# A Fourier layer and eight experts on one core: another order of the experts' model and inner dimensions

## The chip, the cores and the metric

The kernel runs on one core of one Trainium2 chip. The core has a matrix engine (TensorE, PE in the profile, with PEld for its weight loads), a vector engine (VectorE, DVE), a scalar engine (ScalarE, ACT), a general engine (GpSimd, POOL) and a queue that only issues DMAs (SyncE, SP). Matrix products land in PSUM; everything else lies in SBUF, which has 128 partitions. Each engine works through its own list of instructions in a fixed order, and waits for the others by semaphores. The metric is the device time of one execution in microseconds; the time before is the median of three runs.

## What is computed

The reference has two halves. The first mixes a batch of 8 sequences (2496 positions, 256 features) in the frequency domain; the second routes all 19968 tokens to 8 experts of equal capacity and applies each expert's two-layer network.

```python
X = np.fft.rfft(x, axis=1); Xr, Xi = X.real, X.imag
Yr = Xr @ w_r - Xi @ w_i + b_r
Yi = Xr @ w_i + Xi @ w_r + b_i
Yr = sign(Yr) * max(|Yr| - 0.01, 0); Yi = sign(Yi) * max(|Yi| - 0.01, 0)
x = np.fft.irfft(Yr + 1j * Yi, n=2496, axis=1).reshape(19968, 256)

logits = x @ w_gate                          # [19968, 8]
# all (token, expert) pairs in order of falling logit: a token goes to the first
# expert that still has room; each expert takes cap = 19968 / 8 = 2496 tokens
for e in range(8):
    h = np.maximum(x[assigned == e] @ w1[e], 0.0)    # w1[e]: 256 x 1024
    out[assigned == e] = h @ w2[e]                   # w2[e]: 1024 x 256
```

The product of an expert doesn't depend on the order in which the 256 features of x and w1's rows are summed, nor on the order in which the 1024 inner columns are numbered, as long as w1's columns and w2's rows are numbered alike.

## The kernel before

**Stages.** The transform runs batch by batch (`phase_a`), as matrix products with fixed matrices, with transposing steps through DRAM (T1, T2); its result goes to the DRAM tensor YD and its logits to LG. When four batches are done, a router (`Router.early`) finds for each expert up to 512 tokens that will surely be its own: the eight *early lists*. Their experts' products run at the end of the transform and behind it. When all logits are there, `Router.closing` finds, one expert after the other, the expert whose capacity closes next, and the rest of its tokens (1984): the eight *late lists*. Each closing is a search for a threshold: DVE counts (L402 to L407), PE sums the counts over partitions (L412, L413), DVE decides (L430 to L434, L451, L452). There is a slow way, `general`, for inputs on which the certificates of the fast way fail; it isn't run with these inputs.

**A list's work** (`Experts.run`). Tokens are gathered from YD by an indirect DMA (L581), 128 at a time, a token to a partition. `xpose` turns them by PE (L596), so that features lie on partitions: the 256 features are two groups of 128, and the transposing matmul's weight load reads one group of columns. ACT and DVE split the result into a high and a low part (L599, L600). `ffn1` makes the hidden layer, 128 inner columns (ft) and up to 512 tokens at a time, from three products: high times high, high times low, low times high (L611), summed over the two groups of features. ACT and DVE apply the maximum and split again (L614, L615). `ffn2` sums over the eight ft (L627), ACT copies (L630), and an indirect DMA scatters the rows to the output (L634).

**A list's weights** (`Experts.load`). Each of w1 and w2 of an expert comes in two halves of 512 KB into a raw tile of 128 partitions x 1024 words. There are two raw tiles; they lie where the transform had its tile xt, so the profile names them xt. For each half, ACT copies the raw words into the high part (L567) and DVE subtracts the copy from the raw words into the low part (L568), which also frees the raw tile for the next half. w1's parts lie in tiles that the profile names sh, w2's in FG; each has two places, so that one list's weights can be made while another's are in use. Early lists know their expert, and SP loads the halves by plain DMAs (L557). Late lists' experts are known only from the search, so POOL gathers 128 rows of 4 KB by row numbers that DVE makes (wi, L809 to L811), with an indirect DMA (L559); the same two columns of row numbers serve w1 and w2.

**The numbering before.** Half m of w1 has the rows d = 2 p + m on partition p, each 1024 columns long, 4 KB. Inner column f = 8 k + t becomes place k of ft = t, so the two split instructions read the raw row with a step of eight words and write in order. w2's rows f = 8 p + t belong to that: half g has rows 8 p + 4 g to 8 p + 4 g + 3, 4 KB in one piece, in order. The transposes read every second column of the gathered tokens.

**What sets the order.** A planner (`Plan.run`) simulates the whole program with given costs and positions and writes out each engine's order once, at build time. Its costs are numbers in the calls: 0.95 us for the ACT copy (L567) and 0.068 + 1024/960 us for the DVE subtraction (L568), 0.118 us for a transpose, 0.65 us and a tail for a DMA from SP. PE's order thus has the search's little matmuls at fixed places between the experts' matmuls, and DVE's order has the search's counts at fixed places between the experts' splits.

Of the kernel before, what the change touches and what calls it, by code (L numbers as in the profile page):

```python
# [15 lines left out]
OP = mybir.AluOpType  # L16
# [250 lines left out]
class Kit:  # L267
# [17 lines left out]
    def v(self, n, pos, emit, reads, writes): return self.plan.add('V', 0.068 + n / 960, pos, emit, reads, writes)  # L285
# [252 lines left out]
class Experts:  # L538

    def __init__(self, K, H, YD, YDb, w1, w2, out):  # L540
        self.K, self.H, self.YD, self.YDb, self.out = K, H, YD, YDb, out
        self.w = (w1, w2)
        self.rows = (w1.rearrange("e (p m) f -> (e p m) f", m=2), w2.rearrange("e (p g m) d -> (e p g) (m d)", g=2, m=4))
        self.spacer = K.one("spacer_b", [1, 1])
        self.scat = []

    def load(self, pos, e=None, wi=None):

        K, plan, v = self.K, self.K.plan, self.K.v
        W1, W2 = K.sb("W1", [128, 2, 2, 1024], F32R), K.sb("W2", [128, 2, 8, 256], F32R)  # L550
        for k in range(2):
            for m in range(2):
                r = K.sb("raw", [128, 1024])
                p = pos + (2 * k + m)
                if e is not None:
                    src = self.w[k][e].rearrange("(p m) f -> p m f", m=2)[:, m] if not k else self.w[k][e].rearrange("(p g m) d -> p g (m d)", g=2, m=4)[:, m]
                    K.dma(p, lambda r=r, src=src: K.nc.sync.dma_start(r.t, src), 524e3, [], [r])  # L557
                else:
                    K.ind(p, lambda r=r, k=k, m=m: K.P.indirect_dma_start(out=r.t, out_offset=None, in_=self.rows[k],  # L559
                                                                          in_offset=bass.IndirectOffsetOnAxis(ap=wi.t[:, m:m + 1], axis=0)), 524e3, [wi], [r])  # L560

                def part(i, k=k, m=m, r=r):
                    if k: return W2.t[:, i - 1, 4 * m:4 * m + 4] if i else r.t.rearrange("p (m d) -> p m d", m=4)
                    return W1.t[:, i - 1, m].rearrange("p (t k) -> p t k", t=8) if i else r.t.rearrange("p (k t) -> p t k", t=8)
                W = (W1, W2)[k]
                h = plan.buf(None, None)
                plan.add('A', .95, p + 1, lambda part=part: K.A.copy(part(1), part(0)), [r], [W, h])  # L567
                v(1024, p + 1, lambda part=part: K.V.tensor_tensor(part(2), part(0), part(1), op=OP.subtract), [r, h], [W])  # L568
        return W1, W2

    def run(self, n, base, W, gi, go, gs, oi, oo, pos_g, early=False):

        K, H, plan, v = self.K, self.H, self.K.plan, self.K.v
        V, A, P, T = K.V, K.A, K.P, K.T
        W1, W2 = W
        NT, NC = (n + 127) // 128, (n + 511) // 512
        xg, xT, hT = {}, {}, {}
        for t in range(NT):
            if not t % 2: xg[t // 2] = K.sb("xg", [128, 2, 256])
            g = xg[t // 2]  # L580
            q = K.ind(pos_g(t), lambda t=t, g=g: P.indirect_dma_start(  # L581
                out=g.t[:, t % 2], out_offset=None, in_=self.YD[0:EB * S] if early else self.YD, in_offset=bass.IndirectOffsetOnAxis(ap=gi.t[:, go + t:go + t + 1], axis=0)),
                131e3, [gs[t]] + (self.YDb[0:EB] if early else self.YDb), [g])
            gi.users.append(q)

        def xpose(c, pos):
            nt = min(4, NT - 4 * c)
            xT[c] = [[K.sb("xT", [128, 512], F32R) for _ in range(2)] for _ in range(2)]
            for m in range(2):
                h, l = xT[c][m]  # L590
                ps = K.psum("psx", [128, 512])

                def tr(ps=ps, m=m):
                    for q in range(nt):
                        t = 4 * c + q
                        T.transpose(ps.t[:, 128 * q:128 * q + 128], xg[t // 2].t[:, t % 2].rearrange("p (k m) -> p m k", m=2)[:, m], H.idn)  # L596
                K.t(.118 * nt, pos + .5 * m, tr, [H.b_idn] + [xg[t] for t in range(2 * c, 2 * c + (nt + 1) // 2)], [ps])
                w = 128 * nt
                plan.add('A', .052 + w / 1200, pos + .5 * m, lambda ps=ps, h=h: A.copy(h.t[:, 0:w], ps.t[:, 0:w]), [ps], [h])  # L599
                v(w, pos + .5 * m, lambda ps=ps, h=h, l=l: V.tensor_tensor(l.t[:, 0:w], ps.t[:, 0:w], h.t[:, 0:w], op=OP.subtract), [ps, h], [l])  # L600
# [39 lines left out]
        HD, k = 2, base  # L640
# [32 lines left out]
class Router:  # L673
# [56 lines left out]
    def closing(self, i, pos, lo3):  # L730

        K, H, X = self.K, self.H, self.X
        V, T, v = K.V, K.T, K.v
# [4 lines left out]
        ML, m, am, AG, eid, certs, lohi = H.b_ML, H.b_m, H.b_am, H.b_AG, H.b_eid, H.b_certs, H.b_lohi  # L738
# [3 lines left out]
        if i < 7:  # L742
# [14 lines left out]
            rng, r = self.rng, RR[i]  # L757
# [3 lines left out]
            else:  # L761
# [4 lines left out]
                ps = count(K, H, pos, c, no, ag, NJ, "pq", self.junk, self.acc, eqs)  # L766
# [8 lines left out]
            ps = count(K, H, pos, c, no, ag, NJ, "pq", self.junk, self.acc, eqs)  # L775
            f = self.fl[i] = K.sb("fl", [128, 8])
# [6 lines left out]
            wf, g8 = K.sb("wi", [128, 1]), K.sb("g8", [128, 8])  # L783
            v(8, pos(), lambda: V.scalar_tensor_tensor(g8.t[:, 0:no], f.t[:, 0:no], 1.0, eid.t[:, 0:no], op0=OP.mult, op1=OP.mult, accum_out=wf.t), [f, eid], [g8, wf])
            pw = pos()
# [16 lines left out]
        else:  # L802
            wf, pw = K.sb("wi", [128, 1]), pos()
# [2 lines left out]

        v(215, pos(), lambda: V.scalar_tensor_tensor(gl.t, gm.t, 1.0, H.ne, op0=OP.mult, op1=OP.mult, accum_out=cnt.t[:, 0:1]), [gm, H.b_ne], [gl, cnt])
        wa, wi = K.sb("wi", [128, 1]), K.sb("wi", [128, 2], I32)
        v(1, pw, lambda: V.tensor_scalar(wa.t, wf.t, 7.0, 128.0, op0=OP.min, op1=OP.mult), [wf], [wa])  # L809
        v(1, pw, lambda: V.tensor_tensor(wa.t, wa.t, H.pc[:, 0:1], op=OP.add), [wa, H.b_pc], [wa])  # L810
        v(2, pw, lambda: V.scalar_tensor_tensor(wi.t, wa.t.to_broadcast([128, 2]), 2.0, H.iE[:, 0:2], op0=OP.mult, op1=OP.add), [wa, H.b_iE], [wi])  # L811
        ps2 = K.psum("pq", [128, 8])
        K.t(.05, pos(), lambda: (T.matmul(ps2.t[:, 0:1], lhsT=H.tri, rhs=cnt.t[:, 0:1], start=True, stop=True), T.matmul(ps2.t[:, 1:2], lhsT=H.ones, rhs=cnt.t[:, 0:1], start=True, stop=True)), [cnt, H.b_tri, H.b_ones], [ps2])
        v(1, pos() + 5, lambda: V.tensor_scalar(certs.t[:, 8 + i:9 + i], ps2.t[:, 1:2], 1.0 - CAP + EN, None, op0=OP.add), [ps2], [certs])
# [7 lines left out]
        p = pos() + 5  # L822
# [337 lines left out]
def general(tc, nc, H, LG, YD, w1, w2, cR, out):  # L1160
# [4 lines left out]
    with ExitStack() as ctx:  # L1165
        K = Kit(tc, nc, ctx, RINGS)
        plan, V, A, P, T, v, sb, psum = K.plan, K.V, K.A, K.P, K.T, K.v, K.sb, K.psum
# [3 lines left out]
        pc, iE, ones, tri, sml, ML, m, am, AG = H.b_pc, H.b_iE, H.b_ones, H.b_tri, H.b_sml, H.b_ML, H.b_m, H.b_am, H.b_AG  # L1171
# [25 lines left out]
        def closing(i, pos):  # L1197
# [7 lines left out]
            if i < 7:  # L1205
# [31 lines left out]
                for k in range(31, -1, -1):  # L1237
# [10 lines left out]
                    ps = total(cnt)  # L1248
# [5 lines left out]
                ps = total(cnt)  # L1254
# [8 lines left out]

            g8, wf, wi = sb("g8", [128, 8]), sb("wi", [128, 1]), sb("wi", [128, 2], I32)
            v(8, pos(), lambda g8=g8, wf=wf: V.scalar_tensor_tensor(g8.t, wE.t, ec.t[:, 0:1], iE.t, op0=OP.is_equal, op1=OP.mult, accum_out=wf.t), [wE, ec, iE], [g8, wf])
            v(1, pos(), lambda wf=wf: V.scalar_tensor_tensor(wf.t, wf.t, 128.0, pc.t[:, 0:1], op0=OP.mult, op1=OP.add), [wf, pc], [wf])
            v(2, pos(), lambda wf=wf, wi=wi: V.scalar_tensor_tensor(wi.t, wf.t.to_broadcast([128, 2]), 2.0, iE.t[:, 0:2], op0=OP.mult, op1=OP.add), [wf, iE], [wi])
            if i < 7:

                g8a, g8b, g8c = [sb("gw", [128, 8]) for _ in range(3)]  # L1270
# [95 lines left out]
```

## Time and profile before

| | |
|---|---|
| median of three runs | 1635.14 us (1633.94 to 1639.24) |
| the profiled execution | 1637.3 us, span 1635.5 us, mean granted clock 0.984 |
| PE busy | 1543.4 us, 94% of the span |
| DVE busy | 1181.4 us, 72% |
| ACT busy | 882.4 us, 54% |
| POOL busy | 607.8 us, 37% |
| DMA | 210.64 MB, mean 129 GB/s |

One execution was profiled, and its lines are quoted by engine (PE, PEld, DVE, ACT, POOL, SP), source line and the names of the tiles written and read ("sh<-xt" is w1's split). Buffer numbers are left out of the names. "PE a L1 <- DVE b L2: 8.4, 6, 2.3" says that PE stood idle in front of its instructions on tile a at line 1 for 8.4 us in all, six times, at most 2.3 us, until DVE's instruction on b at line 2 ended. A q behind an engine's name means its instruction queue. Matmuls overlap one another, so PE's busy time is a union of overlapping spans.

### The profile page before, as it was taken

How to read it: one execution, taken by the hardware profiler on the slowest of the kernel's cores; microseconds unless marked ns; L12 is line 12 of the kernel's file. 1: busy time of each engine (PE TensorE's matmuls, PEld its weight loads, DVE VectorE, ACT ScalarE, POOL GpSimd, SP SyncE). 2: the span in 40 equal slices, each digit the busy share in tenths (PEclk: the TensorE clock that was granted, in tenths of full speed). 3: DMA queues.
4: the chain of work that ended last, by engine and by line, in shares of the span. 5: the costliest groups of instructions: out<-in, count | busy, mean ns of one | idle time of the engine just before them, and what ended most of it. 6: DMA issues, size and time to landing. Idle time of an engine off the chain costs nothing.

```text
span 1635.5 us, 31215 instructions
## 1 busy us (share of the span) xinstructions
PE 1543.4 (94%) x10980; PEld 1381.9 (84%) x10980; DVE 1181.4 (72%) x3652; ACT 882.4 (54%) x1875; POOL 607.8 (37%) x726
## 2 busy tenths in 40 slices
PE   6999999999999967989899999999999999999997
PEld 3899999998798845878788888888889899889997
DVE  2777777778988885688988989988777766552331
ACT  1568788787688764454634434444344443563331
POOL 1114343343344556212342623534325253473112
PEclk8999999999999988999999999999999999999999
DMA  8877787887686564323221302211122211231000
GB/s 239 237 248 249 224 248 221 251 248 204 216 235 223 165 186 139 113 90 105 90 79 44 101 25 72 71 67 61 44 75 70 72 61 62 84 115 46 20 25 27
DMA packets 134489, 210.64 MB, mean 129 GB/s; under 512 B 31183, under 2 KB 94367, under 8 KB 134129
## 3 DMA queue, kind: packets, MB, share of 16 engines
q1 hardware_dynamic: 112468, 145.53, 29.7%
q0 software_dynamic: 21856, 63.04, 12.3%
q8 instruction: 88, 1.44, 0.4%
q14 instruction: 77, 0.63, 0.1%
HBM read 123.75 MB, written 84.75 MB: 127 GB/s over the span
## 4 chain that ended last, share of the span: by engine, by line
PE 31%; issue 12%; DVE 6%; POOL 4%; ACT 2%; DMA 2%; POOLq 0%; ACTq 0%
PE ps L627 14%; PE ps L611 10%; PE p L611 5%; POOL out_dram L634 3%; DMA xt<-in_moe_w_dram,wi 2%; DVE sh L568 2%; ACT sh L567 1%; PE ps L596 1%; DVE junk L402 1%; DVE FG L568 1%; ACT FG L567 0%; PE p L499 0%; POOL xt L559 0%; DVE yTl L615 0%; ACT ajunk L504 0%
## 5 line engine op out<-in xcount | busy, mean ns | idle before, releaser
L1010 PE MATMUL ps<-wt,xTh 128*128 128x256 f32 x1280 | 242.9, 289 | 0.0
L1010 PEld LDWEIGHTS ps<-wt,xTh 128*128 128x128 f32 x1280 | 200.8, 192 | 2.9 <-issue 0.2
L1010 PE MATMUL ps<-wt,xTl 128*128 128x256 f32 x640 | 181.3, 283 | 0.0
L868 POOL TENSOR_TENSOR s2l<-s2c,s2h 120x512 fp32r<-120x512 f32 (+1 forms) x96 | 118.0, 1233 | 142.7 <-ACT s2h L865 136.5
L634 POOL DMA_INDIRECT out_dram<-xTh,li x64 | 71.2, 1113 | 263.1 <-ACT xTh L630 235.5
L1087 POOL TENSOR_TENSOR yTl<-yr,yTh 128x468 bf16<-128x468 f32 (+1 forms) x88 | 98.8, 1122 | 165.8 <-ACT yTh L1084 114.9
L402 DVE SCALAR_TENSOR_TENSOR junk<-h_m,st,h_AG 128x156 bf16<-128x156 f32 (+1 forms) x472 | 157.9, 380 | 2.5
L1010 PEld LDWEIGHTS ps<-wt,xTl 128*128 128x128 f32 x640 | 122.2, 191 | 0.0
L630 ACT COPY xTh<-ps 128x256 f32<-128x256 f32 x80 | 29.9, 373 | 149.1 <-PE ps L627 127.3
L627 PE MATMUL ps<-FG,yTh 128*128 128x256 f32 (+1 forms) x504 | 108.8, 283 | 0.0
L991 PE MATMUL ps<-FG,sh 128*128 128x128 f32 x640 | 97.0, 282 | 8.4 <-DMA sh<-T 8.0
L991 PEld LDWEIGHTS ps<-FG,sh 128*128 128x128 f32 x640 | 88.4, 195 | 16.5 <-issue 9.5
L630 ACT COPY xTl<-ps 128x256 f32<-128x256 f32 x80 | 29.8, 372 | 126.7 <-PE ps L627 120.6
L634 POOL DMA_INDIRECT out_dram<-xTl,li x64 | 64.9, 1014 | 86.8 <-ACT xTl L630 77.8
L627 PE MATMUL ps<-FG,yTl 128*128 128x256 f32 (+1 forms) x368 | 88.3, 283 | 0.0
L568 DVE TENSOR_TENSOR sh<-xt,sh 128x1024 fp32r<-128x1024 f32 x32 | 69.4, 2182 | 17.9 <-ACT sh L567 17.8
L627 PEld LDWEIGHTS ps<-FG,yTh 128*128 128x128 f32 (+1 forms) x504 | 80.7, 187 | 0.7
L627 PE MATMUL ps<-FG,s2c 128*128 128x256 f32 (+1 forms) x356 | 80.4, 284 | 0.0
L1016 DVE TENSOR_TENSOR ps<-ps,bt 128x512 f32<-128x512 f32 x80 | 55.5, 694 | 30.7 <-PE ps L1010 25.6
L868 DVE TENSOR_TENSOR xl<-xt,xh 117x512 fp32r<-117x512 f32 (+1 forms) x77 | 61.0, 794 | 22.3 <-ACT xh L865 20.2
L1057 PE MATMUL p<-s2h,d 120*117 120x512 f32 (+1 forms) x192 | 76.7, 408 | 0.3 <-DVE s2h L865 0.3
L611 PE MATMUL ps<-y,sh 128*128 128x512 f32 (+1 forms) x187 | 71.5, 400 | 3.6 <-DVE yTl L615 1.6
(648 smaller groups left out, 5162.8 us busy)
## 6 DMA issues: line engine op xcount, KB each, us to landing
sh<-T SPq DMA_DIRECT2D x40, 512.0 KB
T<-s4st SPq DMA_DIRECT2D x80, 256.0 KB
s2c<-T SPq DMA_DIRECT2D x80, 240.0 KB
YD<-yst SPq DMA_DIRECT2D x80, 234.0 KB
T<-s1st SPq DMA_DIRECT2D x73, 240.0 KB
xt<-in_moe_w_dram SPq DMA_DIRECT2D x32, 512.0 KB
xt<-in_x_dram SPq DMA_DIRECT2D x105, 156.0 KB
LG<-lgst SPq DMA_DIRECT2D x80, 21.9 KB
```

What stands on the lines that cost most here:

```text
L402: v(cols + 59, p, lambda k=k: V.scalar_tensor_tensor(junk[k % 2].t[:, 0:cols], H.m[:, 0:cols], c.t[:, k // ng:k // ng + 1], ag(k % ng)[:, ...
L568: v(1024, p + 1, lambda part=part: K.V.tensor_tensor(part(2), part(0), part(1), op=OP.subtract), [r, h], [W])
L611: T.matmul(ps.t[:, 0:w], lhsT=W1.t[:, a, m, 128 * ft:128 * ft + 128], rhs=x_.t[:, 0:w], start=q + m == 0, stop=q + m == 3)
L627: T.matmul(ps.t[0:M], lhsT=a.t[:, 128 * q:128 * q + M], rhs=W2.t[:, w_, ft], start=k == 0, stop=k == 23)
L630: plan.add('A', .27, pos + 1, lambda: A.copy(o.t[0:M], ps.t[0:M]), [ps], [o])
L634: ins = P.indirect_dma_start(out=self.out, out_offset=bass.IndirectOffsetOnAxis(ap=oi.t[0:M, oo + t:oo + t + 1], axis=0), in_=o.t[0:M], in ...
L868: lambda: eng.tensor_tensor(lb[1](), src(), hb[1](), op=OP.subtract), [srcb, hb[0]], [lb[0]])
L991: T.matmul(ps.t[:, i, 128 * dt:128 * dt + 128], lhsT=sh.t[:, k, 128 * dt:128 * dt + 128], rhs=Ft.t[:, k], start=True, stop=True)
L1010: T.matmul(ps3.t[:, i], lhsT=a.t[:, i, dt, o:o + 128], rhs=wt[c].t[:, w, dt], start=n == 0, stop=n == 11)
L1016: plan.add('V', dve(512), pos + 1.282, lambda ps3=ps3: V.tensor_tensor(ps3.t, ps3.t, bt[:, None, :].to_broadcast([128, 2, 256]), op=OP.add ...
L1057: T.matmul(ps.t[0:M, gs_], lhsT=d5[0:k_, a, 0:M], rhs=v.t[0:k_, gs_], start=i == 0, stop=i == 2)
L1087: yq.append(plan.add('P', pool(2 * W), pos + 0.376, lambda yh=yh, yl=yl, yr=yr, W=W: P.tensor_tensor(yl.t[:, :, 0:W], yr.t[:, :, 0:W], yh. ...
```

## The change

Model dimension: half m has the features d = 128 m + p, in place of 2 p + m. Transposes read 128 neighbouring columns; w1's halves are blocks of 128 neighbouring rows.

Inner dimension, late lists: f = 512 g + 4 k + t is place k of ft = 4 g + t. The gathered row of w2, four rows of 1 KB in one piece of 4 KB, is row number 128 g + p of an expert's 256; the split of w1 reads its raw row with a step of four words. So the row number is 256 e + 128 m + p for both weights, made by three instructions as before.

Inner dimension, early lists: in memory order, f = 512 g + 128 t + k. The split of w1 reads its raw row in order; a half of w2 is loaded as four pieces of 1 KB for each partition, rows 512 g + 128 t + p, by the same DMA from SP.

The planner's costs and positions stay. The same edit of the row numbers is made in `general`.

```diff
-        self.rows = (w1.rearrange("e (p m) f -> (e p m) f", m=2), w2.rearrange("e (p g m) d -> (e p g) (m d)", g=2, m=4))
+        self.rows = (w1.rearrange("e d f -> (e d) f"), w2.rearrange("e (r m) d -> (e r) (m d)", m=4))
...
-                    src = self.w[k][e].rearrange("(p m) f -> p m f", m=2)[:, m] if not k else self.w[k][e].rearrange("(p g m) d -> p g (m d)", g=2, m=4)[:, m]
-                    K.dma(p, lambda r=r, src=src: K.nc.sync.dma_start(r.t, src), 524e3, [], [r])
+                    src = self.w[k][e].rearrange("(m p) f -> p m f", m=2)[:, m] if not k else self.w[k][e].rearrange("(g m p) d -> p g m d", g=2, m=4)[:, m]
+                    K.dma(p, lambda r=r, src=src, k=k: K.nc.sync.dma_start(r.t.rearrange("p (m d) -> p m d", m=4) if k else r.t, src), 524e3, [], [r])
...
-                    return W1.t[:, i - 1, m].rearrange("p (t k) -> p t k", t=8) if i else r.t.rearrange("p (k t) -> p t k", t=8)
+
+                    return W1.t[:, i - 1, m].rearrange("p (g t k) -> p g t k", g=2, t=4) if i else r.t.rearrange("p (g k t) -> p g t k" if e is None else "p (g t k) -> p g t k", g=2, t=4)
...
-                        T.transpose(ps.t[:, 128 * q:128 * q + 128], xg[t // 2].t[:, t % 2].rearrange("p (k m) -> p m k", m=2)[:, m], H.idn)
+                        T.transpose(ps.t[:, 128 * q:128 * q + 128], xg[t // 2].t[:, t % 2, 128 * m:128 * m + 128], H.idn)
...
-        v(1, pw, lambda: V.tensor_scalar(wa.t, wf.t, 7.0, 128.0, op0=OP.min, op1=OP.mult), [wf], [wa])
+        v(1, pw, lambda: V.tensor_scalar(wa.t, wf.t, 7.0, 256.0, op0=OP.min, op1=OP.mult), [wf], [wa])
         v(1, pw, lambda: V.tensor_tensor(wa.t, wa.t, H.pc[:, 0:1], op=OP.add), [wa, H.b_pc], [wa])
-        v(2, pw, lambda: V.scalar_tensor_tensor(wi.t, wa.t.to_broadcast([128, 2]), 2.0, H.iE[:, 0:2], op0=OP.mult, op1=OP.add), [wa, H.b_iE], [wi])
+        v(2, pw, lambda: V.scalar_tensor_tensor(wi.t, H.iE[:, 0:2], 128.0, wa.t.to_broadcast([128, 2]), op0=OP.mult, op1=OP.add), [wa, H.b_iE], [wi])
```

More of the change, by code (lines that the diff above doesn't have):

```diff
@@ L1265, in closing @@
             v(8, pos(), lambda g8=g8, wf=wf: V.scalar_tensor_tensor(g8.t, wE.t, ec.t[:, 0:1], iE.t, op0=OP.is_equal, op1=OP.mult, accum_out=wf.t), [wE, ec, iE], [g8, wf])
-            v(1, pos(), lambda wf=wf: V.scalar_tensor_tensor(wf.t, wf.t, 128.0, pc.t[:, 0:1], op0=OP.mult, op1=OP.add), [wf, pc], [wf])
-            v(2, pos(), lambda wf=wf, wi=wi: V.scalar_tensor_tensor(wi.t, wf.t.to_broadcast([128, 2]), 2.0, iE.t[:, 0:2], op0=OP.mult, op1=OP.add), [wf, iE], [wi])
+            v(1, pos(), lambda wf=wf: V.scalar_tensor_tensor(wf.t, wf.t, 256.0, pc.t[:, 0:1], op0=OP.mult, op1=OP.add), [wf, pc], [wf])
+            v(2, pos(), lambda wf=wf, wi=wi: V.scalar_tensor_tensor(wi.t, iE.t[:, 0:2], 128.0, wf.t.to_broadcast([128, 2]), op0=OP.mult, op1=OP.add), [wf, iE], [wi])
             if i < 7:
```

## The prediction

> **What bounds the kernel now.** The page first: its span and the chain that ended last.
>
> ```profile
> span 1635.5 us, 31215 instructions
> PE ps L627 14%; PE ps L611 10%; PE p L611 5%; POOL out_dram L634 3%; DMA xt<-in_moe_w_dram,wi 2%; DVE sh L568 2%; ACT sh L567 1%; PE ps L596 1%; DVE junk L402 1%; DVE FG L568 1%; ACT FG L567 0%; PE p L499 0%; POOL xt L559 0%; DVE yTl L615 0%; ACT ajunk L504 0%
> ```
>
> The chain ends in the experts' matmuls (L611, L627), but "DVE sh L568" and "ACT sh L567" stand in it: the two instructions that split w1 (tile sh) into a high and a low part. The split of w2 (tile FG), of the same size, is at 1% and 0%. So I asked for both lines by form.
>
> ```profile
> L567 ACT CAST sh<-xt x32: 2075/2246/2431, 505.1 to 1426.7; 128x1024 fp32r<-128x1024 f32 x32
> L567 ACT CAST FG<-xt x32: 1037/1048/1112, 570.1 to 1447.1; 128x1024 fp32r<-128x1024 f32 x32
> L568 DVE TENSOR_TENSOR sh<-xt,sh x32: 2003/2186/2354, 507.3 to 1429.0; 128x1024 fp32r<-128x1024 f32 x32
> L568 DVE TENSOR_TENSOR FG<-xt,FG x32: 1205/1225/1950, 574.6 to 1448.2; 128x1024 fp32r<-128x1024 f32 x32
> ```
>
> The same 128x1024 takes 2.25 us on ACT for w1 and 1.05 for w2, on DVE 2.19 and 1.23 (medians). The only difference is the pattern read: w2 in memory order, w1 every eighth word (f = 8 k + t), 32 bytes apart. Each of the 16 lists splits w1 in two halves: 16 halves belong to early lists, 16 to late ones.
>
> Then the stages, by stretches of the span (columns: length, then busy time of PE, weight loads, DVE, ACT, POOL, granted clock, DMA share, GB/s).
>
> ```profile
> 470.00:560.00 90.00, 85.46 (x718) 78.84 (x717) 74.55 (x156) 70.25 (x166) 49.82 (x46) 1.00 0.73 223
> 560.00:640.00 80.00, 58.99 (x409) 44.62 (x409) 62.49 (x112) 47.78 (x104) 48.19 (x42) 0.87 0.53 157
> 640.00:830.00 190.00, 172.75 (x1133) 151.78 (x1132) 153.99 (x537) 98.24 (x162) 58.83 (x79) 0.98 0.33 106
> 830.00:886.00 56.00, 54.97 (x369) 48.61 (x368) 46.67 (x247) 18.86 (x35) 13.90 (x23) 1.00 0.11 35
> 886.00:1480.00 594.00, 581.62 (x3916) 522.23 (x3915) 450.43 (x1804) 270.53 (x640) 253.23 (x332) 1.00 0.22 71
> ```
>
> From 640 to 830, where early lists 3 to 8 run and the first late list gets its weights, PE is idle 190 - 172.75 = 17.25 us. From 830 on it has next to no gap: 1.0 us to 886, and 12.4 in 594 us of late lists. What PE waits for from 640 to 830 (total us, times, longest):
>
> ```profile
> PE pt L412 <- DVE cnt L407: 8.4, 6, 2.3
> PE ps L627 <- DVE zh L615: 3.2, 2, 1.6
> PE ps L627 <- DVE yst L615: 2.8, 2, 1.6
> ```
>
> That is 14.4 of the 17.25 us in ten waits, all for small DVE work that is queued on DVE. What it is queued behind, at one of them (timeline of ACT, DVE, PE):
>
> ```profile
> 696.68 4.58 ACT L567 CAST sh<-xt 128x1024 fp32r<-128x1024 f32 x2 [0.93 <-PE p L611]
> 699.07 4.34 DVE L568 TENSOR_TENSOR sh<-xt,sh 128x1024 fp32r<-128x1024 f32 x2 [1.25 <-ACT sh L567]
> 704.42 0.16 DVE L407 TENSOR_TENSOR cnt<-acc,cnt 128x4 bf16<-128x4 f32 x1
> 704.64 0.18 PE L412 MATMUL pt<-cnt,h_ones 128*128 128x4 bf16 x1 [2.34 <-DVE cnt L407]
> ```
>
> DVE waits 1.25 us for the first ACT copy, then splits two halves for 4.34 us; the router's count comes out at 704.58, and PE, which has the count's matmul next in its order, stands 2.34 us. So in this stage the split of w1 is what ends last, at seven pairs: early lists 3 to 8, and late list 1 near 815. (Early list 1 splits at 505 to 516, list 2 at 588 to 596, late list 2 near 891 and so on.)
>
> **The change, part by part.** No duration given to the planner changes, so every engine keeps its order and no instruction or DMA is added, dropped or moved past a queue. Only durations change.
>
> *w1, early lists: read in memory order.* By the rows of FG, the first ACT copy falls by 2.25 - 1.05 = 1.20 us and the two DVE subtractions by 0.96 each: a pair ends 1.20 + 1.92 = 3.1 us sooner. The longest PE wait is 2.3 us, so each that stands behind an early pair should close. Six of the seven pairs are early; the late one keeps its wait of up to 2.3 us, and I leave 1 us to waits that only happen to end on L407: 11 of the 14.4 us, about the DVE work that goes, 6 x 1.92 = 11.5. Bounds: 6 us (every second copy decides, 6 x 0.96) and 15 (all of PE's idle time but the late wait). What is late next is PE itself, at its matmul rate. Of early list 1 I count nothing, since 470 to 560 has 4.5 us of PE gaps in all. List 2's is on the way to the last logits (timeline of DVE, then PE's waits):
>
> ```profile
> 591.48 4.12 DVE L568 TENSOR_TENSOR sh<-xt,sh 128x1024 fp32r<-128x1024 f32 x2
> 595.52 0.63 DVE L1082 TENSOR_TENSOR yr<-pt,yTh 128x468 f32<-128x468 f32 x1
> PE ps L1098 <- POOL yTl L1087: 1.9, 1, 1.9
> PE ps L1098 <- ACT yTh L1084: 1.4, 1, 1.4
> ```
>
> PE's gate matmuls wait 3.3 us there for work queued behind these copies; DVE gives back 1.9 us. I take 2 (bounds 0 and 3.3).
>
> The gain must pass the stretch 830 to 886. Its last event is the number of the second late list's expert, from a search in which DVE and PE answer each other (DVE's waits from 830 to 890, and POOL's timeline):
>
> ```profile
> DVE g L451 <- PE pt L413: 8.2, 11, 1.2
> 886.50 0.98 POOL L559 DMA_INDIRECT xt<-in_moe_w_dram,wi  x1 [7.99 <-DVE wi L811]
> ```
>
> DVE is busy 46.67 of 56 us there and waits 8.2 for PE, while PE waits for almost nothing: PE sets the pace, and if both come to 830 earlier, all of it is earlier.
>
> *w1, late lists: f = 512 g + 4 k + t, words 16 bytes apart.* No row has this pattern. Its bounds are the two forms above: 2.25 and 2.19 us, or 1.05 and 1.23. A wider stride stands in the maximum over lists, 624 bytes:
>
> ```profile
> L747 DVE TENSOR_REDUCE h_m<-h_ML 128x156 f32<-128x1092 f32 x1 | 2.3, 2314 | 0.0
> L747 DVE TENSOR_REDUCE h_m<-h_ML 128x156 f32<-128x936 f32 x1 | 2.0, 2005 | 0.0
> ```
>
> (2314 - 2005)/156 = 1.98 ns a word, against 2186/1024 = 2.13 at 32 bytes: from 32 to 624 bytes the price stands still, like a fixed price for leaving the neighbourhood of the last word. The nearest row is the 32-byte one, so I take no gain; the other bound is a rival. [...] No run here shows 16 bytes.
>
> *Transposes (L596), 320: columns 128 m on, no longer every second.* The weight load reads them:
>
> ```profile
> L596 PEld LDWEIGHTS ps<-h_idn,y 128*128 128x128 f32 x56 | 9.4, 209 | 0.6 <-issue 0.2
> L991 PEld LDWEIGHTS ps<-FG,sh 128*128 128x128 f32 x640 | 88.4, 195 | 16.5 <-issue 9.5 <-DMA sh<-T 0.8 <-PE p L960 0.8
> ```
>
> 14 ns dearer than L991, which reads neighbours. 320 x 14 ns = 4.5 us at most; loads overlap matmuls, so nothing at least. I take 2, nearly all in the PE-bound stage.
>
> *w2, early lists: four pieces of 1 KB for each of 128 partitions, no longer 4 KB.* 16 DMAs go from 128 pieces to 512. SP's issue price for 512 pieces stands at L351, beside L557's own; then a pair's issue and its use, and the DMA rate where such 4 KB loads run and where the transform's 1 KB rows (T, s2c, YD) do.
>
> ```profile
> L351 SPq DMA_DIRECT2D h_ML<-LG x8: 585/589/687, 180.1 to 650.3; - x8
> L557 SPq DMA_DIRECT2D xt<-in_moe_w_dram x32: 327/328/367, 479.9 to 786.3; - x32
> 675.28 2.36 SPq L557 DMA_DIRECT2D xt<-in_moe_w_dram  x2
> 686.18 2.00 ACT L567 CAST FG<-xt 128x1024 fp32r<-128x1024 f32 x2 [3.14 <-PE ps L627]
> DMA to landing us min/median/max: 3.9/4.8/5.8
> 663.00:668.00 5.00, 4.85 (x25) 3.97 (x24) 4.83 (x12) 2.76 (x7) 3.75 (x4) 1.00 0.65 210
> 240.00:260.00 20.00, 20.00 (x166) 18.78 (x165) 16.93 (x30) 15.52 (x34) 6.57 (x5) 1.00 0.83 229
> ```
>
> SP pays 0.26 us more for each; behind the pair of list 3 (647 us) stand the last batch's logits (L351), 0.5 us later by that and 3.1 sooner because the raw tiles come free sooner. At 210/0.65 = 323 GB/s of full share against 229/0.83 = 276, a pair of 1.05 MB takes 0.5 us longer. It is issued by 677.64 and used at 686.18, released by PE: 8.5 us, where the late lists' loads of the same 512 KB land in 5.8 at most. Covered; cost 0. Without the cover it would be 0.5 to 1 us a list.
>
> *The row numbers (L809 to L811)* are the same three small DVE instructions, with other factors: 0. The late w1 gather fetches 128 neighbouring rows of 4 KB, no longer every second: 0, within the 3.9 to 5.8 us above.
>
> **Sum:** 11 + 2 + 2 = 15 us; by the bounds 6 to 23. The profiled execution took 1637.3 us around its span of 1635.5; 1637.3 - 15 = 1622.3. The median shown, 1635.14, is 2.2 below that execution, so 1620.
>
> **The rivals.** *(a) 16 bytes are as cheap as neighbours.* Then the late lists' pairs also end 3.1 us sooner: 2.3 us at late list 1, and of the 12.4 us of PE gaps among the others, some of which are for transfers and for ACT, 8 us: 1610. For it: nothing here has a stride between 8 and 32 bytes. Against: the flat price from 32 to 624. [...]
>
> *(b) The gain is swallowed at 886.* If the search's DVE work, and not PE, sets the second late list's number, PE arrives 13 us early and stands until the gather at 886. Left are the transposes and little else, 3 us: 1632. For it: DVE is 81% busy from 640 to 830, and busy or waiting all the time from 830. Against: what DVE waits for there is PE, and DVE itself loses 11.5 us of work before 830.
>
> *(c) Slower: the early w2 loads become the bound.* If a piece costs the same whatever its size, a pair takes four times as long on the DMA engines: 1.05 MB at 323 GB/s is 3.3 us, so 13, landing near 690 where ACT wants it at 686 or, sooner now, 683; 4 to 7 us late for six lists is 24 to 42, less 15: about 1653. It decides from 8.5 us between issue and landing on. Against: the row at 240 us, where 1 KB rows move at 276 GB/s of full share.
>
> That memory order doesn't speed the split is hardly a case: FG is the same copy.
>
> **How the numbers follow.** Forecast 57% (own range 1612 to 1629, the bounds), (a) 25%, (b) 13%, (c) 5%. The range runs from 1606 ((a) with all its 14.7 us) to 1631, leaving out (c) and most of (b). About 0.3% (4.9 us) is what can be told from no change here. Faster: 57 + 25 and 3 of (b), 85%; same 10%; slower 5%.
>
> **What would show it.** L567 and L568 on sh should fall apart into 16 at 1.05 and 1.23 us and 16 at about 2.2. PE's idle time in the early stage should fall from 17 to about 6 us, its waits for cnt L407 almost vanish, and the second late list's first gather be issued near 873, not 886.5; the late lists from there should keep their length to 2 or 3 us. Wrong would be: the gather still at 886; sh at 16 bytes below 1.5 us; ACT FG released by a DMA in the early stage; L596 loads still at 209 ns.

## The result and the profile after

The changed kernel takes 1616.59 us (median of four runs, 1611.52 to 1618.58), where the kernel before takes 1635.14. The ratio is 0.9875, with a 95% interval from 0.9855 to 0.9895: faster, by 18.5 us or 1.2% between the medians. The profiled execution took 1618.58 us, 18.7 less than that of before (1637.3).

The page of the changed kernel (its lines are numbered one higher from L567 on: L568 is ACT's copy, L569 DVE's subtraction, L597 the transposes, L612 and L628 the experts' matmuls):

```profile
span 1616.8 us, 31215 instructions
DMA packets 140633, 210.64 MB, mean 130 GB/s; under 512 B 31183, under 2 KB 102559, under 8 KB 140273
PE ps L628 20%; PE ps L612 13%; PE ps L1011 11%; PE p L612 6%; PE ps L992 3%; PE ps L1028 3%; PE p L961 3%; PE p L1058 2%; POOL out_dram L635 2%; DMA xt<-in_moe_w_dram,wi 2%; PE ps L597 1%; PE pt L1078 1%; DVE junk L402 1%; DMA sh<-in_x_dram 1%; DVE sh L569 1%
```

The chain still ends in the experts' matmuls, now with more of them in it; "ACT sh" has left the list and "DVE sh" is down from 2% to 1%. The count of instructions is the same. The packets are 6144 more than the 134489 of before: 16 early w2 loads with 384 more pieces each.

The two split instructions of w1, first from 470 to 830 us, then from 850 to 1500 us (duration in ns: lowest, median, highest):

```profile
L568 ACT CAST sh<-xt x18: 1040/1049/2050, 504.9 to 794.1; 128x1024 fp32r<-128x1024 f32 x18
L569 DVE TENSOR_TENSOR sh<-xt,sh x18: 1201/1223/2093, 506.2 to 796.2; 128x1024 fp32r<-128x1024 f32 x18
...
L568 ACT CAST sh<-xt x14: 2040/2078/2127, 871.3 to 1405.6; 128x1024 fp32r<-128x1024 f32 x14
L569 DVE TENSOR_TENSOR sh<-xt,sh x14: 1987/2018/2065, 882.2 to 1407.7; 128x1024 fp32r<-128x1024 f32 x14
```

The 18 of the first stretch are the 16 early halves and the two of the first late list. The early ones fell to what w2's cost, 1.05 and 1.22 us. The late ones, now with a step of 16 bytes, still take 2.08 and 2.02 us.

The stages, over stretches that hold the same work as those shown of before (columns as there):

```profile
636.10:810.70 174.60, 168.91 (x1132) 148.51 (x1131) 141.84 (x537) 82.89 (x162) 58.50 (x79) 0.99 0.37 115
...
810.70:866.00 55.30, 54.23 (x366) 47.86 (x365) 46.18 (x243) 18.80 (x35) 13.86 (x23) 1.00 0.11 35
866.00:1460.00 594.00, 580.30 (x3910) 518.77 (x3909) 447.79 (x1809) 266.96 (x638) 252.54 (x332) 1.00 0.22 71
```

The work that took 190 us from 640 on takes 174.6. PE is idle 5.7 us in it (17.25 before), and its busy time fell as well, from 172.75 to 168.91. The search after it takes 55.3 us for 56, and the late lists have the same 594 us with the same gaps (13.7 us for 12.4). PE's waits from 636 to 812 us:

```profile
PE pt L412 <- DVE cnt L407: 2.4, 2, 1.6
PE ps L612 <- DVE yTl L616: 1.8, 2, 1.1
PE p L499 <- ACT jl L505: 1.2, 1, 1.2
```

The six waits for cnt, 8.4 us, have become two, 2.4 us together, and those at the second product for zh and yst (6.0 us) are gone. At the place shown of before (count at 704.42, PE 2.34 us late) the timeline of the changed kernel has:

```profile
687.48 2.00 ACT L568 CAST sh<-xt 128x1024 fp32r<-128x1024 f32 x2 [0.93 <-PE p L612]
688.56 2.36 DVE L569 TENSOR_TENSOR sh<-xt,sh 128x1024 fp32r<-128x1024 f32 x2
691.94 0.16 DVE L407 TENSOR_TENSOR cnt<-acc,cnt 128x4 bf16<-128x4 f32 x1
692.93 0.18 PE L412 MATMUL pt<-cnt,h_ones 128*128 128x4 bf16 x1
```

From the start of ACT's pair to the count it was 7.74 us and is 4.46, which is 3.3 us less; the count is there at 692.10, and PE comes for it 0.8 us later without having waited.

Last, the search at the second late list: POOL's timeline and DVE's waits from 812 to 870 us.

```profile
866.93 0.98 POOL L559 DMA_INDIRECT xt<-in_moe_w_dram,wi  x1 [7.92 <-DVE wi L812]
```

```profile
DVE g L451 <- PE pt L413: 8.1, 11, 1.2
```

The gather is issued 19.6 us earlier than at 886.50, and DVE waits for PE there as before (8.1 us in eleven waits): the search moved as a whole.

PE's order is the same in all kernels here that keep the planner's input, so the n-th matmul of one trace can be set against the n-th of another. How much earlier the same matmul starts than in the profile of before (us; the columns are the time in the trace of before, the last one is the last matmul):

| kernel | 500 | 560 | 640 | 680 | 720 | 760 | 820 | 880 | 1100 | 1440 | 1460 | end |
|---|---|---|---|---|---|---|---|---|---|---|---|---|
| changed | 0.2 | 1.0 | 4.0 | 9.3 | 13.2 | 17.2 | 19.3 | 19.6 | 19.2 | 21.2 | 18.4 | 18.7 |
| early order alone (e1) | 0.7 | 3.4 | 5.2 | 10.8 | 14.8 | 18.6 | 21.6 | 21.6 | 21.7 | 22.8 | 22.8 | 22.8 |
| early lists at 16 bytes (e2) | -0.3 | 1.3 | 3.6 | 5.2 | 7.4 | 8.6 | 8.4 | 8.6 | 9.9 | 11.1 | 11.2 | 11.5 |
| early w2 in 1 KB pieces alone (e3) | -0.3 | -1.7 | 0.2 | 0.2 | 0.1 | 0.1 | 0.2 | 0.1 | 0.3 | 0.2 | 0.3 | 0.3 |
| late w1 in order too (e4) | 0.8 | 3.4 | 5.7 | 10.7 | 14.6 | 18.6 | 24.1 | 24.3 | 28.5 | 36.0 | 36.0 | 36.4 |

Four microseconds come before 640, 15.3 from 640 to 820, and on balance nothing afterwards (the fall from 21.2 to 18.4 between 1440 and 1460 is in this row alone). Each row is one trace. Those of e1 and e4 are of the fastest execution of their kernel (1614.59 and 1600.91 us), that of the changed kernel is of the slowest of its four, so the rows tell where time is gained, and the medians tell how much.

### The profile page after: what moved, and what is told of

It reads as the page before. It is cut to its first block, busy times and chain, and to the rows that moved or that the text cites. A ratio compares the mean times of both kernels' runs of the same rounds, so it can differ in the third digit from the quotient of the medians.

```text
span 1616.8 us, 31215 instructions
## 1 busy us (share of the span) xinstructions
PE 1541.9 (95%) x10980; PEld 1376.9 (85%) x10980; DVE 1164.1 (72%) x3652; ACT 860.3 (53%) x1875; POOL 607.1 (38%) x726
## 4 chain that ended last, share of the span: by engine, by line
PE 66%; DVE 11%; issue 10%; DMA 6%; ACT 3%; POOL 3%; SPq 0%; POOLq 0%; DVEq 0%; ACTq 0%
PE ps L628 20%; PE ps L612 13%; PE ps L1011 11%; PE p L612 6%; PE ps L992 3%; PE ps L1028 3%; PE p L961 3%; PE p L1058 2%; POOL out_dram L635 2%; DMA xt<-in_moe_w_dram,wi 2%; PE ps L597 1%; PE pt L1078 1%; DVE junk L402 1%; DMA sh<-in_x_dram 1%; DVE sh L569 1%
## 5 line engine op out<-in xcount | busy, mean ns | idle before, releaser
L628 PE MATMUL ps<-FG,yTh 128*128 128x256 f32 (+1 forms) x504 | 108.6, 283 | 0.0
L992 PE MATMUL ps<-FG,sh 128*128 128x128 f32 x640 | 96.7, 282 | 7.5 <-DMA sh<-T 7.5
L992 PEld LDWEIGHTS ps<-FG,sh 128*128 128x128 f32 x640 | 88.3, 195 | 15.5 <-issue 9.6
L628 PE MATMUL ps<-FG,yTl 128*128 128x256 f32 (+1 forms) x368 | 87.8, 282 | 0.0
L628 PEld LDWEIGHTS ps<-FG,yTh 128*128 128x128 f32 (+1 forms) x504 | 80.5, 186 | 0.7
L628 PE MATMUL ps<-FG,s2c 128*128 128x256 f32 (+1 forms) x356 | 80.2, 283 | 0.0
L869 DVE TENSOR_TENSOR xl<-xt,xh 117x512 fp32r<-117x512 f32 (+1 forms) x77 | 61.0, 795 | 20.8 <-ACT xh L866 18.6
L612 PE MATMUL ps<-y,sh 128*128 128x512 f32 (+1 forms) x187 | 71.9, 402 | 3.4 <-DVE s2c L616 1.8
L628 PE MATMUL ps<-FG,y 128*128 128x256 f32 (+1 forms) x328 | 74.0, 284 | 0.0
```

Of the source, the lines that this page charges most:

```text
L612: T.matmul(ps.t[:, 0:w], lhsT=W1.t[:, a, m, 128 * ft:128 * ft + 128], rhs=x_.t[:, 0:w], start=q + m == 0, stop=q + m == 3)
L628: T.matmul(ps.t[0:M], lhsT=a.t[:, 128 * q:128 * q + M], rhs=W2.t[:, w_, ft], start=k == 0, stop=k == 23)
L869: lambda: eng.tensor_tensor(lb[1](), src(), hb[1](), op=OP.subtract), [srcb, hb[0]], [lb[0]])
L992: T.matmul(ps.t[:, i, 128 * dt:128 * dt + 128], lhsT=sh.t[:, k, 128 * dt:128 * dt + 128], rhs=Ft.t[:, k], start=True, stop=True)
```

## The experiments

The first four ran on one chip, where the kernel before took 1639.09 us.

**e1: the early lists' inner order alone.** The kernel before, with early w1 read in order and early w2 in the 1 KB pieces that belong to it; the transposes, the row numbers and the late lists stay as they were.

```
-w2[e].rearrange("(p g m) d -> p g (m d)", g=2, m=4)     # early lists
+w2[e].rearrange("(g m p) d -> p g m d", g=2, m=4)
-r.t.rearrange("p (k t) -> p t k", t=8)
+r.t.rearrange("p (k t) -> p t k" if e is None else "p (t k) -> p t k", t=8)
```

> The kernel before, with the early lists' inner dimension alone put in memory order (w1 read in order, w2 in 1 KB pieces); model dimension and late lists as before. Theory (the early split sets the gain): sh splits fall apart into 16 at 1.05 and 1.23 us and 16 at 2.2; PE's idle time from 640 to 830 us of the span falls from 17 to below 8 us; 15 to 16 of the 18.5 us, ratio 0.990 to 0.991. Rival (the model dimension's order gives most of it, by transposes and w1's rows): 3 us or less, ratio 0.998 or more.

Measured: 1619.06 us (1614.59 to 1620.53), ratio 0.9884, interval 0.9848 to 0.9921. The same work as above, and PE's waits from 640 to 830 us:

```profile
635.00:808.50 173.50, 167.75 (x1134) 148.73 (x1132) 142.32 (x537) 83.33 (x162) 59.71 (x79) 1.00 0.37 116
```

```profile
PE pt L412 <- DVE cnt L407: 2.9, 2, 2.2
```

What follows: the early lists' order is the change. The ratio is a little below the 0.990 to 0.991 that was expected, which lies within the interval, and PE's idle time is 5.75 us, below the 8 expected. The ratio can't be told from the whole change's; what the transposes and the 16-byte step of the late lists add is below what these runs resolve.

**e2: the early lists numbered like the late ones.** The changed kernel, but with all lists at f = 512 g + 4 k + t, a step of 16 bytes, and w2 in pieces of 4 KB.

```
-r.t.rearrange("p (g k t) -> p g t k" if e is None else "p (g t k) -> p g t k", g=2, t=4)
+r.t.rearrange("p (g k t) -> p g t k", g=2, t=4)         # and w2: "(g p m) d -> p g (m d)"
```

> The changed kernel, with the early lists numbered like the late ones: w1 read with a step of 16 bytes, w2 in 4 KB rows. Theory: early ACT copies at 2.08 us and DVE at 1.99, a pair 0.57 us shorter than before and not 3.1; what is left is 3 us of transposes (320 x 10 ns) and 2 to 3 us of pairs, ratio 0.996 to 0.997. Rival (model dimension): the ratio stays at 0.988 to 0.990.

Measured: 1630.12 us, ratio 0.9953, interval 0.9931 to 0.9975. All 32 halves, then PE's waits from 640 to 830 us:

```profile
L568 ACT CAST sh<-xt x32: 2038/2072/2095, 505.4 to 1415.6; 128x1024 fp32r<-128x1024 f32 x32
L569 DVE TENSOR_TENSOR sh<-xt,sh x32: 1981/2017/2068, 507.5 to 1417.7; 128x1024 fp32r<-128x1024 f32 x32
```

```profile
PE pt L412 <- DVE cnt L407: 6.0, 5, 1.8
PE ps L628 <- DVE zh L616: 2.7, 2, 1.5
PE ps L628 <- DVE yst L616: 2.1, 2, 1.5
```

What follows: the expectation, 0.996 to 0.997, held within the interval, and its rival, 0.988 to 0.990, fell. At 16 bytes the splits are 0.17 to 0.18 us shorter than at 32 bytes (2.07 for 2.25 on ACT), and most of PE's waits stay, each a little shorter. With the transposes' part, 0.5% of the time is gained without memory order; the change has 1.25%.

**e3: the early w2 in 1 KB pieces alone.** The kernel before, with only those 16 loads cut; w2's rows then don't match w1's columns.

```
-w2[e].rearrange("(p g m) d -> p g (m d)", g=2, m=4)
+w2[e].rearrange("(g m p) d -> p g m d", g=2, m=4)
```

> The kernel before, with the early w2 halves loaded as four pieces of 1 KB and nothing else; w1 is numbered as before, so w1's columns and w2's rows of the early lists do not belong together in this kernel. Theory: 0.5 us a pair longer on the DMA engines, hidden behind 8.5 us; ratio 0.999 to 1.001. Rival: the loads come late, 0.5 to 1 us a list, 4 to 8 us, ratio 1.0025 to 1.005.

Measured: 1638.77 us, ratio 1.0, interval 0.998 to 1.0019. PE's stage is as before:

```profile
640.00:830.00 190.00, 172.78 (x1134) 151.84 (x1132) 154.01 (x537) 97.87 (x162) 58.86 (x79) 0.98 0.34 106
648.00:655.00 7.00, 5.36 (x27) 4.87 (x28) 2.09 (x2) 0.77 (x3) 2.17 (x4) 0.76 0.79 221
```

What follows: four times as many pieces cost nothing that shows (ratio 1.0) where the load has its 8.5 us, and a trace repeated with the same splits differs from that of before by at most 1.7 us anywhere in the table above, which bounds what its other rows can say. The second row is used further down.

**e4: the late lists' w1 read in order too.** The changed kernel; the late lists' columns are then not numbered like w2's rows.

```
-r.t.rearrange("p (g k t) -> p g t k" if e is None else "p (g t k) -> p g t k", g=2, t=4)
+r.t.rearrange("p (g t k) -> p g t k", g=2, t=4)
```

> The changed kernel, with the late lists' w1 also read in memory order; their w2 rows stay gathered as they are, so w1's columns and w2's rows of the late lists do not belong together in this kernel. It prices what cheap late splits would give. Theory (the late split stands in PE's way at late list 1 and at some of the later boundaries): 3 to 8 us below the changed kernel, ratio 0.983 to 0.986. Rival (gathers and the search set the boundaries): as the changed kernel, 0.9865 to 0.9885.

Measured: 1604.78 us, ratio 0.9797, interval 0.9761 to 0.9833. The changed kernel was not run beside it; by the two ratios (0.9875 there) e4 is some 12 us below it.

```profile
L568 ACT CAST sh<-xt x32: 1038/1049/1057, 504.3 to 1391.3; 128x1024 fp32r<-128x1024 f32 x32
L569 DVE TENSOR_TENSOR sh<-xt,sh x32: 1200/1221/1227, 505.6 to 1392.5; 128x1024 fp32r<-128x1024 f32 x32
```

```profile
886.00:1480.00 594.00, 590.32 (x4006) 532.50 (x4005) 422.11 (x1733) 249.27 (x606) 241.29 (x334) 1.00 0.22 69
```

PE's gaps in the late stage fall to 3.7 us, and 4.8 us come at the first late list (19.3 to 24.1 at 820 in the table). What follows: the late lists' split does stand on the path, from the first late list to the last (24.1 us at 820, 28.5 at 1100, 36.0 at 1440, where the changed kernel stays between 19.2 and 21.2). The 3 to 8 us expected were too few, and the rival, that gathers and the search set the boundaries, fell. The split gained nothing in the change only because 16 bytes were hardly cheaper than 32 (2.08 and 2.02 us for 2.25 and 2.19).

The next four ran on another chip, where the kernel before took 1712.76 us; the times of the two chips are not compared here, only the durations of instructions and the ratios.

**e5: other steps.** The changed kernel with a step of 8 bytes for the late lists and of 64 bytes for the early ones (numbered for the price of the read alone; w2's rows don't match).

```
+late:  r.t.rearrange("p (h k t) -> p h t k", h=4, t=2)
+early: r.t.rearrange("p (k t) -> p t k", t=16)
```

> The changed kernel with two other steps in the read of w1, to price them: late lists with a step of 8 bytes, early lists with a step of 64 bytes; w1's columns and w2's rows do not belong together in this kernel. [...] Rival (the price grows with the step): 8 bytes between, 1.3 to 1.7 us, and 64 bytes above 2.4.

Measured: one run, 1690.03 us. From 500 to 830 us (16 halves at 64 bytes, two at 8), then from 880 on, all at 8 bytes:

```profile
L569 ACT CAST sh<-xt x18: 1094/2008/2086, 505.2 to 808.1; 128x1024 fp32r<-128x1024 f32 x18
L570 DVE TENSOR_TENSOR sh<-xt,sh x18: 1217/1952/2055, 507.3 to 810.8; 128x1024 fp32r<-128x1024 f32 x18
...
L569 ACT CAST sh<-xt x14: 1111/1134/1167, 890.1 to 1464.0; 128x1024 fp32r<-128x1024 f32 x14
L570 DVE TENSOR_TENSOR sh<-xt,sh x14: 1216/1223/1226, 900.9 to 1465.2; 128x1024 fp32r<-128x1024 f32 x14
```

What follows: with 8 bytes the price is nearly gone, 1.13 us on ACT (1.05 in order) and none on DVE (1.22 and 1.22); from 16 to 64 bytes it is nearly one price, 1.95 to 2.25 us. The author's estimates were 1.05 us on ACT and 1.2 on DVE for 8 bytes, and 2.2 for 64; they held, but for 64 bytes at 2.01 us on ACT and 1.95 on DVE, and the rival, a price that grows with the step, fell. Why the price sets in between 8 and 16 bytes is not shown.

**e6: the step on the writing side.** The changed kernel with the late lists' split reading in order and writing words 512 bytes apart, to the same numbering.

```
-W1 "p (g t k) -> p g t k", r "p (g k t) -> p g t k"
+W1 "p (g t k) -> p g k t", r "p (g k t) -> p g k t"     # late lists
```

> The changed kernel; the late lists' split reads its raw row in order and writes w1's tiles with a step of 512 bytes, the numbering unchanged. ACT then has one strided operand, the write; DVE has the copy as a strided read and a strided write. Theory (the price stands on reads alone): ACT 1.05 us, DVE 2.0 as before; the first copy of a late pair 1 us sooner, 1 to 3 us in all, 1613 to 1617 us. Rival (a strided write costs the same): ACT 2.0 and DVE 2.0 or more, no gain.

Measured: one run, 1690.66 us; late halves from 850 us on:

```profile
L568 ACT CAST sh<-xt x14: 2045/2091/2299, 882.7 to 1466.6; 128x1024 fp32r<-128x1024 f32 x14
L569 DVE TENSOR_TENSOR sh<-xt,sh x14: 1947/2028/2276, 893.6 to 1468.7; 128x1024 fp32r<-128x1024 f32 x14
```

What follows: the expectation, that reads alone pay, fell. ACT's copy has its step on the write alone and takes 2.09 us, where the strided read took 2.08. DVE's subtraction has the step twice, in its read of the copy and in its write, and takes 2.03 us, so the second strided operand added nothing there. Moving the step to the other side is no way out here.

**e7 and e8: which of the two halves counts.** The changed kernel, with the early w1 at the old step of 32 bytes in ACT's copy alone (e7) or in DVE's subtraction alone (e8; its low part then belongs to other places than the high part).

```
e7  K.A.copy(W1[:, 0, m] as "p (t k) -> p t k", r as "p (k t) -> p t k")      # t=8
e8  K.V.tensor_tensor(W1[:, 1, m] as "p (t k) -> p t k", r as "p (k t) -> p t k", W1[:, 0, m], subtract)
```

> The changed kernel; early lists' ACT copy of w1 alone reads with the old step of 32 bytes, DVE reads in order, so the parts do not belong together in this kernel. Theory by the terms (first copy 1.20, two subtractions 1.92 of 3.1 us a pair): where DVE's queue decides, 60 to 100% of the pairs' gain stays; early stage (640 to 820 us) gives 9 to 15 us of its 15, ratio 0.988 to 0.9925. Rival (ACT's copy is what matters, DVE waits for it): less than half stays, ratio 0.993 or more.

> The changed kernel; early lists' DVE subtraction of w1 alone reads the raw words with the old step of 32 bytes, ACT copies in order, so the parts do not belong together in this kernel. Theory: only the first ACT copy is shorter, 1.20 of 3.1 us a pair; 40% of the pairs' gain or less stays, ratio 0.993 to 0.996. Rival (ACT decides): most stays, ratio 0.9875 to 0.990.

Measured: 1701.72 us, ratio 0.993 (0.9905 to 0.9955), and 1695.89 us, ratio 0.9915 (0.9884 to 0.9947). e7 lies on the bound of its rival (0.993 or more), e8 between its two expectations. The intervals overlap each other, and the changed kernel itself hadn't run on this chip. That left the question open; both were run again beside it, on a third chip, where the kernel before took 1716.18 us.

> The changed kernel itself, beside the three others on one chip. Both theories: its ratio to the kernel before as measured first, 0.9875, from 0.985 to 0.990.

> The changed kernel with ACT's copy of the early w1 read and written 32 bytes apart as before the change, DVE's subtraction in order. The prediction counts 1.20 us a pair for ACT and 1.92 for DVE, and took DVE's as the gain. Theory (DVE's two subtractions are the gain): within 3 us of the changed kernel. Rival (ACT's copies count in full, because DVE stands until the second one is there): at least 8 us above the changed kernel.

> The changed kernel with DVE's subtraction of the early w1 read and written 32 bytes apart as before the change, ACT's copy in order. Theory (DVE's two subtractions are the gain): at least 8 us above the changed kernel. Rival (ACT's copies count in full): within 3 us of it.

(e10 is e7, e11 is e8.) Measured: the changed kernel 1691.67 us (1688.59 to 1693.45), ratio 0.9866, interval 0.9835 to 0.9897, as on the first chip; e10 1695.77 (1691.44 to 1697.23), ratio 0.9893, interval 0.9865 to 0.9921; e11 1694.08 (1688.76 to 1703.55), ratio 0.9894, interval 0.9857 to 0.993. The first gather of the late lists, in POOL's timeline of the changed kernel, e10 and e11:

```profile
787.34 1.73 POOL L559 DMA_INDIRECT xt<-in_moe_w_dram,wi  x1 [4.86 <-DVE FG L569]
```

```profile
792.04 1.73 POOL L559 DMA_INDIRECT xt<-in_moe_w_dram,wi  x1 [4.87 <-DVE FG L569]
```

```profile
791.08 1.73 POOL L559 DMA_INDIRECT xt<-in_moe_w_dram,wi  x1 [4.86 <-DVE FG L569]
```

What follows: e10 is 4.1 us above the changed kernel, between its two expectations (within 3, at least 8). e11 is 2.4 us above, which is its rival's side by the median, but its runs spread over 15 us. So the whole time decides nothing here, and the stage must be asked. With one half at the old price the end of the early stage comes 4.7 or 3.7 us later. The two traces stood 2.5 and 2.3 us ahead of the changed kernel's at 640 us, so from there the old copy costs some 7.2 us and the old subtraction some 6.1: each half of the split carries about half of the stage's gain. These are estimates from one trace each. In the whole time that shows only as 2 to 4 us.

**e9: a step of 8 bytes for the late lists, everything computed.** f = 256 h + 2 k + t. The late split reads with the step of 8 bytes that e5 priced. In exchange w2 comes in rows of 2 KB: two gathers for each half, and four more row numbers. The planner is given these, so the order of the engines changes too: of PE's 10980 instructions 3134 stand at another place.

```
+W1 "p (h t k) -> p h t k", r "p (h k t) -> p h t k"      # h = 4, t = 2, late lists
+w2.rearrange("e (r m) d -> (e r) (m d)", m=2)            # rows 512 e + 128 h + p
+for j in range(2): gather r[:, 512 j : 512 j + 512]      # was one gather of 4 KB rows
```

> The changed kernel with the late lists' inner dimension as 256 h + 2 k + t: the split reads words 8 bytes apart, and the expert's w2 is gathered in rows of 2 KB, four gathers for each list where there were two. Everything is computed. Theory (the late split's price is paid once for each leap out of 16 bytes, and stands on the path): w1's late copies take 1.13 us on ACT and 1.22 on DVE, as in the run with 8 bytes, and the whole comes within 3 us of the run that read the late lists in order, about 12 us under the changed kernel beside it. Rival (the two added gathers of each list, about 1 us each on POOL, delay the lists' own gathers and scatters by as much): no better than the changed kernel, up to 2 us for each of eight lists worse.

Measured, beside the changed kernel (a1) on the third chip: 1683.64 us (1674.59 to 1691.62, six runs) for 1691.67; ratio to before 0.9823, interval 0.9787 to 0.9859. Late halves, and the gathers' count:

```profile
L569 ACT CAST sh<-xt x14: 1105/1138/1187, 883.0 to 1458.8; 128x1024 fp32r<-128x1024 f32 x14
L570 DVE TENSOR_TENSOR sh<-xt,sh x14: 1214/1224/1226, 893.9 to 1460.1; 128x1024 fp32r<-128x1024 f32 x14
...
L560 POOL DMA_INDIRECT xt<-in_moe_w_dram,wi x48: 946/978/1777, 783.3 to 1474.6; - x48
```

What follows: the splits fall to the price of e5 (1.14 us on ACT and 1.22 on DVE), and 16 more gathers of 1 us on POOL don't take it back: the median is 8.0 us below the changed kernel's, two thirds of e4's gain. The expectation, within 3 us of the 12, missed by about 1 us, and the rival, no better than the changed kernel, is not borne out by the median. What the new order adds or takes is not separated from the split, and the two intervals overlap, so 8 us is an estimate. By its median it is the fastest here of the kernels that compute everything. The theory's 16 bytes are a reading of the steps that were run (ACT's copy took 1.13 us at 8 bytes, 2.08 at 16, 2.25 at 32, 2.01 at 64); how the price comes about is not shown.

## Why the prediction was right, and by how much its terms were off

The forecast was 1620 us, with a range from 1606 to 1631; 1616.59 came out, and no rival's condition held. The direction, the place and the mechanism held; the sum was 15 where the profiles differ by 18.7.

**Early w1, 11 us: right in mechanism, too small.** 15.4 us came from this stage (190 to 174.6), just over the upper bound of 15. Of that 11.6 us are PE's idle time, 17.25 to 5.7: that is the term, and the forecast "17 to about 6". What the step left out is the other 3.8 us: PE's busy time for the same matmuls fell from 172.75 to 168.91, and in e1 to 167.75, where the transposes are untouched. Part of that is the granted clock, 0.98 in the stretch before, 0.99 and 1.00 in these two. It fell to one half for 3.4 us at a time: in this stage twice before, once in the changed kernel, never in e1. First the two of before, then the one of the changed kernel:

```profile
651.30:654.70 3.40, 3.40 (x15) 3.12 (x14) 0.00 (x0) 0.37 (x1) 2.15 (x4) 0.50 0.96 255
705.90:709.30 3.40, 3.40 (x15) 3.11 (x15) 1.61 (x10) 0.58 (x2) 2.25 (x4) 0.50 0.13 46
```

```profile
784.00:787.40 3.40, 3.40 (x11) 2.38 (x10) 3.40 (x16) 1.98 (x8) 2.48 (x4) 0.50 0.73 245
```

If half the clock is half the work, 3.4 us at 0.50 do that of 1.7, an estimate from the granted clock alone. What the traces show: 14 matmuls that start one behind the other from 651.29 us on took 3.54 us before, up to the start of the next, and the same 14 took 1.99 in the changed kernel, from 644.96 on at 1.00, which is 1.55 us less. By the estimate the clock makes 1.7 of the changed kernel's 3.8 us, and 3.4 of e1's 5.0; the rest of both is not accounted for. One place shows gap and clock together, 648 to 655 us in the trace of before, and 644 to 651 in the changed kernel's, which is 4 us ahead there:

```profile
648.00:655.00 7.00, 5.23 (x26) 4.66 (x26) 2.31 (x2) 0.97 (x3) 2.15 (x4) 0.76 0.77 222
```

```profile
644.00:651.00 7.00, 7.00 (x56) 6.74 (x55) 1.34 (x3) 1.32 (x4) 3.22 (x6) 1.00 0.79 201
```

Before, PE stands for 1.8 us and then has the half clock, 0.76 in the mean of the 7 us (e3 repeats both, 5.36 us busy and 0.76); in the changed kernel it has neither, and 56 matmuls stand in 7 us for 26. That the gap costs the clock is not shown. Both drops of before begin about 1 us after the end of a PE gap, of 1.6 and of 2.3 us; but four more gaps of 1.6 to 2.3 us in the same stage are followed by none, nor is one of 2.2 us in e1, and in e2, with a gap of 1.5 us at 645 us, the clock stays at 1.00. So the bound "all of PE's idle time" was too low because PE's busy time fell as well.

**The split's price, 1.20 and 0.96 us a half.** Right to 0.02 us. The working took DVE's 11.5 us as the size of the gain and ACT's copies as cover; e10 and e11 show that the two halves weigh about the same.

**List 2's pair, 2 us.** At 640 the changed kernel is 4.0 us ahead. But so is e2, by 3.6, whose splits are only 0.17 us shorter, and the single shifts up to there scatter by up to 1.7 us in e3. The sum of what comes before 640 has the forecast's sign; how much of it is the pair, and of what the rest is made, stays open.

**Late lists, 0.** Right: from the second late list's gather to the end of the span it was 1635.5 - 886.50 = 749.0 us, and is 1616.8 - 866.93 = 749.9. The flat price from 32 to 624 bytes, read from the rows of before, did reach down to 16 (2.08 and 2.02 us), and a step of 64 took 2.01 and 1.95 (e5). It ends below 16: 1.13 and 1.22 us at 8 bytes, for 1.05 and 1.22 in order.

**Transposes, 2 us: not resolved, and reasoned from the wrong row.** The prediction held L596's 209 ns against L991's 195 and called 14 ns the price of every second column. What the changed kernel shows (weight loads by form: busy us and mean ns of one; of L597 two of fourteen groups):

```profile
L992 PEld LDWEIGHTS ps<-FG,sh 128*128 128x128 f32 x640 | 88.3, 195 | 15.5 <-issue 9.6 <-PE p L961 0.5
...
L1078 PEld LDWEIGHTS pt<-h_idn,yst 117*128 117x128 f32 x294 | 34.3, 144 | 12.0 <-DVE yr L1083 3.9 <-ACT jl L505 1.9 <-DVE g L451 1.1
...
L597 PEld LDWEIGHTS ps<-h_idn,y 128*128 128x128 f32 x56 | 7.6, 152 | 1.5 <-DVE zl L601 0.6 <-ACT s4st L1030 0.2 <-DMA y<-YD,li 0.2
...
L597 PEld LDWEIGHTS ps<-h_idn,s1st 128*128 128x128 f32 x32 | 4.2, 141 | 1.0
```

The loads fell to 141 to 152 ns, by some 60 ns and not by 14; the right peer was the other transpose, L1078, at 144. Why L992, which reads neighbours too, takes 195 stays open. 320 times 60 ns are 19 us of weight loads, nearly all of it under matmuls: e1, without this part, is not measurably slower. The 2 us can be neither confirmed nor refuted.

**w2 in 1 KB pieces, 0.** Right, by e3. SP's own price was put too high: 0.26 us more was expected for each load of 512 pieces. The median of L557, half of whose loads are w1's with 128 pieces as before, went from 328 to 378 ns; taken one by one the 16 of w2 took 378 to 409 ns, at most some 0.08 us more.

```profile
L557 SPq DMA_DIRECT2D xt<-in_moe_w_dram x32: 340/378/449, 479.9 to 766.2; - x32
```

**The row numbers, 0.** The gather's 7.92 us of waiting for wi (7.99 before) shows no change.

**The rivals.** (b) fell with the gather at 866.93 and DVE's 8.1 us of waits for PE, unchanged: PE sets the pace of the search. It came 6 us earlier than the forecast's 873, by the 4.4 us that the early stage gave more (15.4 for 11) and the 2 us more before 640. (c) fell with e3. Of (a), the condition fell (2.08 us at 16 bytes, for 1.05 in order) but the price held: 2.3 + 8 us were set for late lists that split as fast as memory order, and e4 measured about 12.

## What to carry to other kernels

Look in the profile for the same instruction on the same shape at two prices; the cheaper twin prices the other access pattern without a run (here w2's 1.05 and 1.23 us were w1's 1.05 and 1.22 afterwards), and the gain is then read from the waits behind it, not from the busy time. Check that the waits are all: here PE's own busy time for the same work fell too (172.75 to 168.91 us). An index order that is free to choose (here the inner dimension of a two-layer network) should be chosen so that the longest elementwise pass takes small steps on both of its sides: here a read with a step of 8 bytes was nearly as good as memory order (1.13 us on ACT for 1.05), one of 16 as bad as one of 64 (2.08 and 2.01), and a step of 512 bytes on the writing side cost the same (2.09). Where small results for PE are queued behind large elementwise work, shortening that work closed PE's gaps here (17.25 us to 5.7): six pairs, each 3.1 us shorter, gave 15.4 us.

## What the runs showed that was not expected

- A step of 16 bytes cost as much as one of 64 (ACT 2.08 and 2.01 us, DVE 2.02 and 1.95, for 1024 words a partition), one of 32 a little more (2.25 and 2.19), one of 8 almost nothing (1.13 and 1.22, for 1.05 and 1.22 in order).
- ACT paid the same on the writing side: 2.09 us with words written 512 bytes apart. DVE took 2.03 us with a strided read and a strided write together, no more than with one.
- A transposing matmul's weight load of every second column took 199 to 210 ns (means of L596's groups before), of neighbouring columns 140 to 152 (L597 in the changed kernel).
- The granted clock fell to one half (0.50) for 3.4 us at a time in the middle of dense work, twice in the early stage before, once in the changed kernel and not at all in e1, with no PE gap in that stage longer than 2.34 us.
